# A fused attention and token-mixing kernel: first tiles loaded in halves, the ones of V written by GpSimd, longer planned transfers, another written order

## The chip, the cores and the metric

One Trainium2 chip, one core. The time is device microseconds of the whole program; the runs of a kernel agree within a fraction of a per cent. Shown times are medians of unprofiled runs. One further execution was recorded by the hardware profiler, and all rows below come from it. Engines: PE is TensorE's matmul stream and PEld its weight loads, DVE is VectorE, ACT is ScalarE, POOL is GpSimd, SP is SyncE, which only issues transfers here.

## What is computed

One sequence of 2048 tokens of width 512 in bf16. After a layer norm without weights, 32-head attention (16 values per head) and a token-mixing MLP (2048 tokens to 1376 and back) are computed side by side and added to the input:

```python
x = A_x
xn = _layernorm(x, axis=-1)
return x + _A_ref(xn, A_wqkv, A_wo) + _B_ref(xn, B_w1, B_b1, B_w2, B_b2)

# _A_ref, in short
q, k, v = heads of x @ wqkv            # 32 heads of 16
p = softmax(q @ k.T * 16 ** -0.5)      # over 2048 keys
return (p @ v) @ wo
# _B_ref, in short
h = _layernorm(x)
u = gelu(einsum("bsd,sf->bdf", h, w1) + b1)
return transpose(einsum("bdf,fs->bds", u, w2) + b2)
```

## The kernel before

**Blocks and groups.** Attention is cut into 32 blocks: 4 stretches of 512 queries by 8 sets of four heads. A block has 16 groups, one for each 128 keys; a group is four score matmuls (four heads, packed in the rows of the array, L557). There are 512 groups.

**Two ways for the exponential.** A group either goes to ScalarE, as two exponentials over 128x1024 (L565), or to VectorE, which builds the exponential out of the bits of a bf16 number: four instructions (one per head) write a first plane from the scores (`dve_first`, L612), and two more add a shift to the whole plane to give a second and a third plane (`add_plane`, L617). The planes together approximate the power of two. The product with V (L577) then takes four matmuls for a ScalarE group and three times four for a VectorE group, the third plane with weights scaled by 0.75 (V17b). V has a seventeenth column of ones beside each head's sixteen values, so that the same matmul sums the denominators; the ones are written once, at the start, by ScalarE (L407).

**A block's end.** When all products of a block stand in their PSUM bank, VectorE copies them (OT, L1093), so that the bank is free for the next block. A chain of small transfers on SP then takes the denominator rows to DRAM (`gather`), back in another layout (`gather2`), VectorE takes reciprocals (L1108), and they go out to DRAM and back, broadcast to four times 32 partitions (`bcast`). GpSimd multiplies the block by them (L1130). Blocks of odd number are joined into the same tile by four more transfers (`join`).

**The start.** Four x tiles of 128 tokens are loaded first, tile 0 and 2 by SP and tile 1 and 3 by ACT's queue (L401); then the first columns of the K and Q weights, then the rest. VectorE takes statistics of tile 0, 1 and 2 (L443, L445), GpSimd the power -1/2 (L453, L455), VectorE normalizes tile 0 (L463), takes tile 3's statistics and normalizes the others; TensorE transposes (L631), ScalarE or VectorE copies them out (L492, L494), TensorE projects K and Q for these tiles (L498), and the first scores and exponentials run while the other 12 tiles are prepared. Matmuls on zeros (L671, L1577) fill TensorE where the planner finds nothing else for it.

**A written order.** The program has no order of its own at run time: when it is built, a planner (class `Sched` and the dispatcher from L1696 on) walks a planned time, with an occupied time (`occ`) and a time to the result (`lat`) for each operation, and writes each engine's instructions in the order that comes out. Engines then run their lists in order and wait on semaphores. Which groups go to VectorE, and where each filler stands, falls out of this walk. `TOL` says by how much work put in between may make ScalarE's scores late; `JOIN` how long TensorE may wait for a VectorE bank, so that its scores go out together with ScalarE's; `KEEP0` how many matmul units TensorE is to have had in the last 3.4 us of planned time up to `T_KEEP0`, with zeros filled in otherwise. The planner also keeps GpSimd's long operations (`occ` above 1000, `wide`) and VectorE's plane steps and normalizations (`two`) apart: a GpSimd operation waits for the last such VectorE operation written before it, and VectorE's list places none inside a long GpSimd operation's planned time. Nothing makes VectorE wait for GpSimd at run time in this: if GpSimd starts later than planned, they run side by side.

**The tail.** After the last block VectorE transposes its sums, divides, and transposes back (L1734 to L1741), TensorE adds the output projection of the last pieces (L899, L907, L934), ScalarE and VectorE copy out four tiles, and SP stores them. Projection steps that don't need the last block are written into the list from the point at which the block before the last is planned to have been multiplied.

Of the kernel before, what the change touches and what calls it, by code (L numbers as in the profile page):

```python
# [8 lines left out]
ACTF = mybir.ActivationFunctionType  # L9
# [5 lines left out]
D = 512  # L15
H = 32
# [7 lines left out]
NKT = 16  # L24
# [233 lines left out]
def bass_parallel_sum__softmax_full_mha__mixer_token_mlp__prompt_kernel(  # L258
# [11 lines left out]
    x = A_x  # L270
    if len(x.shape) == 3:
        x2 = x.rearrange("b s d -> (b s) d")
        out2 = out.rearrange("b s d -> (b s) d")
    else:
        x2, out2 = x, out

    with ExitStack() as es:
# [8 lines left out]
        x_sb = x_flat[:, :].rearrange("p (t d) -> p t d", d=D)  # L286
# [10 lines left out]
        KT = sb("KT", [128, 4, S], BF16)  # L297
# [37 lines left out]
        PV_BANK = 6  # L335
# [21 lines left out]
        NPRE = 4  # L357
        TABLE = 1283.0


# [29 lines left out]
        def ld_x(a, b_, lat, q="sp"):  # L390
            dma(q, x_sb[:, a:b_, :],
                x2[128 * a:128 * b_, :].rearrange("(t p) d -> p t d", p=128),
                reads=[], writes=[("x", t) for t in range(a, b_)], name="ld_x", lat=lat)
# [7 lines left out]
        for t in range(NPRE):  # L401
            ld_x(t, t + 1, 2150 + 200 * (t // 2), "sp" if t % 2 == 0 else "act")
        ld_w(1, 0, 1, 3000, "sp")
        ld_w(0, 0, 1, 3100)
        sc.add("act", lambda e: e.activation(r2[:, 0:1], zw[:, 0:1], ACTF.Identity), reads=[("zw",)], writes=[("r2",)],
               occ=1500)
        sc.add("act", lambda e: e.activation(v17_views[0][1][:, :, 16], KT[:, 1, 0:NKT * H], ACTF.Identity, bias=1.0),  # L407
               reads=[("KTt", 1, t) for t in range(4)], writes=[("Vone",)], occ=490, lat=670)
        ld_x(4, 6, 4500)
# [32 lines left out]
        def ln_stats1(t):  # L442
            sc.add("dve", lambda e: e.bn_stats(stats[:, t, :], x_sb[:, t, :]),  # L443
                   reads=[("x", t)], writes=[("stats", t)], occ=650, lat=780)
            return sc.add("dve", lambda e: e.bn_aggr(mv[:, t, 0:2], stats[:, t, :]),  # L445
                          reads=[("stats", t)], writes=[("mv", t)], occ=105, lat=232)
# [242 lines left out]
        transpose_mm(2, 0, 0)  # L689
        ln_norm(3)  # L690
        xnT_evac(2, 1, 0, 0, "dve")
        qt0_mm(0, QB)
# [393 lines left out]
        def chain_epi(b):  # L1086
# [16 lines left out]
            def gather2():  # L1103
                return dma("sp", den_s[:, eb, :], den_dram[eb].rearrange("r (c e) -> (r c) e", e=16),
                           reads=[("dend", eb)], writes=[("den_s", eb)], name="den_i", noncontig=True, lat=3000)

# [8 lines left out]
            def bcast():  # L1115
                assert bc_done[0] == b
                bc_done[0] += 1
                for r in range(4):
                    op = dma("sp", denb[32 * r:32 * r + 32, :], rec_dram[eb][r:r + 1, :].broadcast_to([32, 512]),
                             reads=[("recd", eb)], writes=[("denb", r)], name="den_b", noncontig=True, lat=2500)  # L1120
                return op
# [288 lines left out]
        def pv_candidates(t):  # L1410
            b = pv_block[0]
            if b >= NBLK or not pv_open[0]:
                return []
            return [it for it in pv_items[b] if it[0] <= t and (
                b > 0 or (it[2] % NKT in (v0_done if it[1] == "A" else v0b_done) and v_ready(it) <= t))]
# [25 lines left out]

        TOL = 150.0
        JOIN = 45.0
        DEFER = 250.0
# [3 lines left out]
        def pe_fill(t, lim, same_cfg):  # L1448
            cands = []
            pvc = pv_candidates(t)  # L1450
            if pvc and sc.ready(writes=[("bank", PV_BANK)], eng="pe") <= t:
                it = min(pvc, key=lambda z: (z[1] == "D" and len(planes_avail()) > 1, z[0]))
                cands.append(("P", it))
# [137 lines left out]
        KEEP = 8.0  # L1591
        KEEP0, T_KEEP0 = 12.0, 25000.0
        n_zero = [0]
# [11 lines left out]

        D_HUNGRY = 0.0
        FAR = 1300.0
        n_act_ = [0]
# [233 lines left out]
```

## Time and profile before

| | us |
|---|---|
| median of three unprofiled runs | 698.42 |
| lowest and highest of them | 698.36, 699.23 |
| profiled execution | 701.9 |
| its span, first to last instruction | 700.1 |
| ScalarE busy | 683.0 |
| VectorE busy | 657.8 |
| TensorE busy (matmul stream) | 657.4 |
| GpSimd busy | 64.3 |

How to read the rows: a group of instructions stands as line, engine, operation, tile written, tile read, shapes and count, then busy time, the mean of one in ns, and the idle time of that engine just before these instructions, with what ended most of it. Instructions of one engine overlap at their ends, so the mean of one can be longer than its share of the busy time. A row of a timeline has the start, the length, the engine and line, how many instructions are merged, and in brackets the idle time before. The granted clock of TensorE is 1.00 at full speed and 0.50 when it is throttled.

### The profile page before, as it was taken

The page shows a single profiled execution, that of the slowest core. Times are in us where ns is not written, and L with a number is a line of the kernel's source. Part 1 is how long each engine was busy: PE and PEld are TensorE (multiplying, and loading weights), DVE is VectorE, ACT ScalarE, POOL GpSimd, SP SyncE. Part 2 cuts the span into 40 slices and gives each one's busy share as a digit, 9 for nine tenths or more (in the row PEclk, how much of TensorE's full clock was granted, in tenths as well). Part 3 has the DMA queues.
Part 4 walks back from the last instruction along what each step waited for, and adds up shares of the span by engine and source line. Part 5 has one row for each costly group of instructions (what it writes and reads, how often), then busy time and mean ns, then how long its engine had stood idle before and what let it go on. Part 6 is the DMA issues. An engine that isn't in the chain of part 4 may idle for free.

```text
span 700.1 us, 15532 instructions
## 1 busy us (share of the span) xinstructions
PE 657.4 (94%) x6195; PEld 198.4 (28%) x6277; DVE 657.8 (94%) x1139; ACT 683.0 (98%) x742; POOL 64.3 (9%) x93
## 2 busy tenths in 40 slices
PE   8999999999999999999999999989989999999987
PEld 4533333322222222222222222222222222222222
DVE  7888999999999999999999999998999999999997
ACT  7999999999999999999999999998999999999995
POOL 4510100000000000000000000000000000001000
PEclk9999999999999999999999999998999999999999
DMA  7024110022223221011222211111100122211001
GB/s 211 1 68 82 37 26 11 20 47 58 46 51 73 48 58 40 23 32 37 54 62 49 63 52 48 47 44 44 37 23 15 32 52 60 58 45 44 15 9 45
DMA packets 78367, 32.65 MB, mean 47 GB/s; under 512 B 63004, under 2 KB 74204, under 8 KB 78296
## 3 DMA queue, kind: packets, MB, share of 16 engines
q1 hardware_dynamic: 77480, 31.27, 18.4%
q8 instruction: 49, 0.80, 0.5%
q10 hardware_dynamic: 816, 0.39, 0.2%
q14 instruction: 22, 0.18, 0.1%
HBM read 26.08 MB, written 2.61 MB: 41 GB/s over the span
## 4 chain that ended last, share of the span: by engine, by line
ACT 84%; PE 9%; DVE 4%; issue 1%; POOL 0%; DMA 0%; DVEq 0%
ACT pT L565 83%; PE ps L557 3%; PE ps L577 3%; DVE x_sb L612 1%; PE ps L889 1%; ACT gT L880 1%; DVE plx L612 1%; PE ps L498 1%; DVE x_sb L617 1%; PE ps L899 1%; POOL r L480 0%; DMA x_sb<-in_A_x_dram 0%; DVE stats L443 0%; PE ps L631 0%; ACT QT L518 0%
## 5 line engine op out<-in xcount | busy, mean ns | idle before, releaser
L565 ACT ACTIVATE pT<-ps 128x1024 bf16<-128x1024 f32 x726 | 667.8, 1136 | 5.2 <-PE ps L557 4.9
L557 PE MATMUL ps<-QT,KT 32*128 32x512 bf16 x2048 | 291.0, 385 | 21.7 <-ACT pT L565 18.5
L612 DVE TENSOR_SCALAR x_sb<-ps 128x512 int16<-128x512 f32 x268 | 183.3, 686 | 12.0 <-PE ps L557 3.3
L612 DVE TENSOR_SCALAR plx<-ps 128x512 int16<-128x512 f32 x272 | 178.5, 682 | 3.6 <-PE ps L557 3.2
L557 PEld LDWEIGHTS ps<-QT,KT 32*128 32x128 bf16 x2048 | 73.9, 91 | 282.6 <-ACT pT L565 265.5
L577 PE MATMUL ps<-pT,V 128*32 128x512 bf16 x1452 | 143.6, 391 | 0.9 <-DVE OT L1093 0.6
L617 DVE TENSOR_SCALAR x_sb<-plx 128x2048 int16<-128x2048 int16 x90 | 61.3, 685 | 0.9 <-PE ps L577 0.6
L577 PEld LDWEIGHTS ps<-pT,V 128*32 128x32 bf16 x1452 | 36.5, 93 | 80.5 <-issue 74.3
L577 PE MATMUL ps<-plx,V 128*32 128x512 bf16 x556 | 54.0, 386 | 0.4
L577 PE MATMUL ps<-x_sb,V 128*32 128x512 bf16 x532 | 52.1, 388 | 1.7 <-DVE OT L1093 1.3
L889 PE MATMUL ps<-gT,w2blk 128*128 128x512 bf16 (+1 forms) x154 | 50.6, 385 | 3.1 <-issue 2.5
L858 PE MATMUL ps<-h_sb,w1blk 128*128 128x512 bf16 (+1 forms) x157 | 49.1, 385 | 2.7 <-issue 2.5
L1130 POOL TENSOR_TENSOR oT<-OT,denb 128x512 bf16<-128x512 f32 x16 | 20.3, 1271 | 337.0 <-DVE x_sb L617 173.6
L617 DVE TENSOR_SCALAR plx<-x_sb 128x2048 int16<-128x2048 int16 x71 | 48.7, 687 | 2.5 <-PE ps L577 2.2
L1130 POOL TENSOR_TENSOR otmp<-OT,denb 128x512 bf16<-128x512 f32 x15 | 19.1, 1271 | 263.3 <-DMA denb<-rec_scr 100.4
L498 PE MATMUL ps<-xnT,wqkv_sb 128*128 128x512 bf16 (+1 forms) x166 | 35.2, 305 | 3.6 <-issue 1.9
L577 PE MATMUL ps<-x_sb,V17b 128*32 128x512 bf16 x380 | 37.5, 385 | 0.5 <-issue 0.5
L617 DVE TENSOR_SCALAR x_sb<-x_sb 128x2048 int16<-128x2048 int16 x51 | 34.7, 686 | 1.4 <-PE ps L577 1.3
L612 DVE TENSOR_SCALAR xn_sb<-ps 128x512 int16<-128x512 f32 x48 | 32.9, 686 | 2.7 <-PE ps L557 0.8
L617 DVE TENSOR_SCALAR plx<-plx 128x2048 int16<-128x2048 int16 x32 | 21.9, 685 | 1.1 <-PE ps L577 0.8
L1093 DVE COPY OT<-ps 128x512 f32<-128x512 f32 x31 | 21.1, 680 | 0.1
L498 PE MATMUL ps<-wqkv_sb,xnT 128*128 128x128 bf16 x256 | 21.0, 220 | 0.2 <-issue 0.2
(103 smaller groups left out, 371.2 us busy)
## 6 DMA issues: line engine op xcount, KB each, us to landing
denb<-rec_scr SPq DMA_DIRECT2D x124, 64.0 KB, 2.1
w1blk<-in_B_w_dram SPq DMA_DIRECT2D x10, 512.0 KB, 4.1
w2blk<-in_B_w_dram SPq DMA_DIRECT2D x16, 320.0 KB, 3.4
xres<-in_A_x_dram SPq DMA_DIRECT2D x16, 128.0 KB, 2.4
QT<-qst SPq DMA_DIRECT2D x120, 16.0 KB, 1.8
out_dram<-osb SPq DMA_DIRECT2D x14, 128.0 KB, 1.7
wqkv_sb<-in_A_wqkv_dram SPq DMA_DIRECT2D x3, 384.0 KB, 7.6
x_sb<-in_A_x_dram SPq DMA_DIRECT2D x2, 512.0 KB, 6.9
```

Of the source, the lines that this page charges most:

```text
L498: return sc.add("pe", lambda e: e.matmul(dst, lhsT=lhsT, rhs=rhs, start=(ct == 0), stop=(ct == NCT - 1)), reads=reads, writes=[("bank", bk ...
L557: return sc.add("pe", lambda e: e.matmul(bank(bk), lhsT=KT[32 * r:32 * r + 32, T, 128 * kt:128 * (kt + 1)], rhs=QT[32 * r:32 * r + 32, slo ...
L565: return sc.add("act", lambda e: e.activation(pT[:, buf, :], ps[:, slot * 1024:(slot + 1) * 1024], ACTF.Exp, scale=EXP_SCALE), reads=[("ba ...
L577: return sc.add("pe", lambda e: e.matmul(bank(PV_BANK)[32 * r:32 * r + 32, :], lhsT=vt_[:, off:off + 32], rhs=rhs, start=start, stop=stop, ...
L612: return sc.add("dve", lambda e: e.tensor_scalar(plane_i[pb][:, 512 * r:512 * (r + 1)], bank(bk), BIAS, 0.0, ALU.add, ALU.max), reads=[("b ...
L617: return sc.add("dve", lambda e: e.tensor_scalar(plane_i[pb], plane_i[pb0], float(SHIFT[j]), BITS_MAX, ALU.add, ALU.min), reads=[("pl", pb ...
L858: op = sc.add("pe", lambda e: e.matmul(bank(xb)[0:m, :], lhsT=w1blk[:, slot, st, 0:m], rhs=h_sb[:, st, :], start=(st == 0), stop=(st == NT ...
L880: op = sc.add("act", lambda e, m=m, f0=f0, f1=f1: e.activation(gT[0:m, f0:f1, :], gT[0:m, f0:f1, :], ACTF.Gelu_apprx_tanh), reads=[("gT", ...
L889: op = sc.add("pe", lambda e: e.matmul(bank(xb), lhsT=w2blk[0:m, slot, ft, :], rhs=gT[0:m, ft, :], start=first, stop=last), reads=([("w2bl ...
L899: return sc.add("pe", lambda e: e.matmul(bank(bk), lhsT=oT[:, par, T, 128 * sti:128 * (sti + 1)], rhs=wo_c[:, T, :], start=first, stop=las ...
L1093: op = sc.add("dve", lambda e: e.tensor_copy(OT32[:, eb, :], bank(PV_BANK)), reads=[("bank", PV_BANK)], writes=[("OT32", eb)], **T_DVE(512))
L1130: op = sc.add("pool", lambda e: e.tensor_tensor(dst, OT32[:, eb, :], denb[:, :], ALU.mult), reads=[("OT32", eb)] + [("denb", r) for r in r ...
```

## The change

Each of the first four x tiles is loaded as two transfers of 64 partitions, the upper half by SP and the lower by ACT's queue, with a key of its own for the lower half, which the statistics now also wait for. ScalarE's activation that writes the ones of V is removed; a GpSimd memset of the same positions is written after the last of the first four normalizations. The planned landing of the denominators' second transfer goes from 3000 to 3500 ns and of the broadcast from 2500 to 3000 ns. `TOL` goes from 150 to 115, `JOIN` from 45 to 80, and `T_KEEP0` from 25000 to 70000 ns. Three more margins for the products with V (`PVM`, `PLM`, `PAM`) are added and set to zero. As the planner writes the order of all engines from these numbers, the whole order and the split of the groups can come out differently.

```diff
+        LAT_I, LAT_B = 3500.0, 3000.0
...
         for t in range(NPRE):
-            ld_x(t, t + 1, 2150 + 200 * (t // 2), "sp" if t % 2 == 0 else "act")
+            for i, q in enumerate(("sp", "act")):
+                dma(q, x_sb[64 * i:64 * i + 64, t, :], x2[128 * t + 64 * i:128 * t + 64 * i + 64, :], reads=[],
+                    writes=[("x", t)] if i == 0 else [("xh", t)], name="ld_x", lat=2150 + 150 * t)
...
-        sc.add("act", lambda e: e.activation(v17_views[0][1][:, :, 16], KT[:, 1, 0:NKT * H], ACTF.Identity, bias=1.0),
-               reads=[("KTt", 1, t) for t in range(4)], writes=[("Vone",)], occ=490, lat=670)
...
-                   reads=[("x", t)], writes=[("stats", t)], occ=650, lat=780)
+                   reads=[("x", t), ("xh", t)], writes=[("stats", t)], occ=650, lat=780)
...
         ln_norm(3)
+        sc.add("pool", lambda e: e.memset(v17_views[0][1][:, :, 16:17], 1.0), writes=[("Vone",)], occ=2300)
...
-                           reads=[("dend", eb)], writes=[("den_s", eb)], name="den_i", noncontig=True, lat=3000)
+                           reads=[("dend", eb)], writes=[("den_s", eb)], name="den_i", noncontig=True, lat=LAT_I)
...
-                             reads=[("recd", eb)], writes=[("denb", r)], name="den_b", noncontig=True, lat=2500)
+                             reads=[("recd", eb)], writes=[("denb", r)], name="den_b", noncontig=True, lat=LAT_B)
...
-            return [it for it in pv_items[b] if it[0] <= t and (
+            return [it for it in pv_items[b] if it[0] + (PLM if it[1] == "D" else PAM) <= t and (
...
-        TOL = 150.0
-        JOIN = 45.0
+        TOL = 115.0
+        JOIN = 80.0
...
-            if pvc and sc.ready(writes=[("bank", PV_BANK)], eng="pe") <= t:
+            if pvc and sc.ready(writes=[("bank", PV_BANK)], eng="pe") + PVM <= t:
...
-        KEEP0, T_KEEP0 = 12.0, 25000.0
+        KEEP0, T_KEEP0 = 12.0, 70000.0
...
+        PVM, PLM, PAM = 0.0, 0.0, 0.0
```

## The prediction

> **What bounds the kernel now.** I read the page's totals first, then the groups of ScalarE, then its instructions in order of time.
>
> ```profile
> span 700.1 us, 15532 instructions
> ...
> PE 657.4 (94%) x6195; PEld 198.4 (28%) x6277; DVE 657.8 (94%) x1139; ACT 683.0 (98%) x742; POOL 64.3 (9%) x93
> ...
> L565 ACT ACTIVATE pT<-ps 128x1024 bf16<-128x1024 f32 x726 | 667.8, 1136 | 5.2 <-PE ps L557 4.9
> ```
>
> The profiled execution took 701.9 us, 1.8 more than its span. ScalarE does 726 exponentials in 667.8 us, so 0.920 us each (the mean of 1.136 overlaps its neighbours), and has almost no idle time between them. A group of a block is two exponentials on ScalarE, or six instructions and no exponential on VectorE. The end is therefore the first exponential's start, plus 0.920 us for each, plus the gelu, plus the gaps, plus the tail. The gaps are few:
>
> ```profile
> 11.04 7.57 ACT L565 ACTIVATE pT<-ps 128x1024 bf16<-128x1024 f32 x8
> 19.00 9.27 ACT L565 ACTIVATE pT<-ps 128x1024 bf16<-128x1024 f32 x10 [0.39 <-PE ps L557]
> 29.02 280.13 ACT L565 ACTIVATE pT<-ps 128x1024 bf16<-128x1024 f32 x305 [0.75 <-PE ps L557]
> ...
> 471.59 1.02 ACT L565 ACTIVATE pT<-ps 128x1024 bf16<-128x1024 f32 x1 [1.45 <-PE ps L557]
> 473.10 1.02 ACT L565 ACTIVATE pT<-ps 128x1024 bf16<-128x1024 f32 x1 [0.49 <-PE ps L557]
> 474.61 1.02 ACT L565 ACTIVATE pT<-ps 128x1024 bf16<-128x1024 f32 x1 [0.49 <-PE ps L557]
> 476.55 215.09 ACT L565 ACTIVATE pT<-ps 128x1024 bf16<-128x1024 f32 x234 [0.92 <-PE ps L557]
> 695.76 1.09 ACT L492 ACTIVATE osb<-ps 128x512 bf16<-128x512 f32 x2 [4.12 <-PE ps L907]
> ```
>
> Four gaps between 470 and 477 us add up to 1.45 + 0.49 + 0.49 + 0.92 = 3.35 us; two near 19 and 29 us make 1.14. The last exponential ends at 691.64, 8.5 us before the span's end. What happened at 470 stands in the timeline around it and in the table by stretches:
>
> ```profile
> 466.17 1.27 POOL L1130 TENSOR_TENSOR otmp<-OT,denb 128x512 bf16<-128x512 f32 x1 [20.73 <-DMA denb<-rec_scr]
> 466.43 1.55 DVE L617 TENSOR_SCALAR xn_sb<-plx 128x2048 int16<-128x2048 int16 x1
> ...
> 470.39 0.11 PEld L577 LDWEIGHTS ps<-x_sb,V 128*32 128x32 bf16 x4 [1.33 <-DVE OT L1093]
> ```
>
> ```profile
> 75.00:469.00 394.00, 381.78 (x3553) 109.33 (x3596) 377.25 (x628) 393.51 (x426) 24.14 (x19) 1.00 0.19 45
> 469.00:477.00 8.00, 6.96 (x54) 1.30 (x53) 5.58 (x9) 4.66 (x6) 0.00 (x0) 0.57 0.04 9
> 477.00:690.00 213.00, 194.19 (x1883) 55.39 (x1903) 206.05 (x345) 212.90 (x233) 17.46 (x15) 1.00 0.15 37
> ```
>
> (Columns: length; busy time of PE, PEld, DVE, ACT, POOL; granted clock; DMA.) GpSimd's multiply waited for its denominators' transfer, started late, and ran beside a VectorE plane step, which took 1.55 us in place of 0.68. VectorE's copy of the finished block (L1093) came late, TensorE stood 1.33 us for it, its granted clock fell to a mean of 0.57, and ScalarE starved for 3.35 us.
>
> That is the key to the two times. 701.9 - 3.35 = 698.55 lies 0.13 from the median 698.42 of the unprofiled runs. So I take it that those runs mostly don't have this stall: it depends on when a transfer lands. The sum below is made on the profile without its stall, which agrees with the median, and a repaired stall gains nothing there.
>
> The Trainium skill's page "TensorE: Matmul & The Clock Gate" (Part 1: The HAM clock gate) lets the clock fall to half after an idle window of about 3.4 us. The trace differs: the pause was 1.33 us and the clock fell. By the page only the first wait of 1.45 would be lost, by the trace 3.35.
>
> **The start.** Now x tile 0 goes whole on SP and tile 1 whole on ACT's queue at the same moment.
>
> ```profile
> 0.74 0.90 ACTq L350 DMA_DIRECT2D x_sb<-in_A_x_dram  x2
> ...
> 3.61 0.69 DVE L443 BATCH_NORM_STATS2 stats<-x_sb 128x6 f32<-128x512 bf16 x1 [2.39 <-DMA x_sb<-in_A_x_dram]
> ...
> 4.44 0.66 DVE L443 BATCH_NORM_STATS2 stats<-x_sb 128x6 f32<-128x512 bf16 x1
> ```
>
> ```profile
> GB/s 0 0 0 0 0 0 0 0 0 0 0 0 0 0 0 0 0 0 0 0 0 0 0 27 55 68 150 164 164 259 287 314 314 246 300 273 287 232 232 219
> DMA packets 287, 0.27 MB, mean 90 GB/s; under 512 B 24, under 2 KB 287, under 8 KB 287
> ```
>
> (DMA view of the first 3 us; slices of 0.075 us.) By 3.0 us 0.27 MB have moved, about both tiles of 0.13 MB; half of it was there by the slice that ends at 2.48. With tile 0's halves ahead on both queues, tile 0 is complete some 0.5 us earlier, and VectorE's chain, which then runs without a DMA wait, with it: -0.5. Tile 1 is issued one slot of 0.45 us (0.90 for two) later and is wanted 0.83 us after tile 0 (3.61 to 4.44), so it isn't late. The first weights stand behind the same number of bytes on each queue as before.
>
> The Trainium skill's page "DMA: Bandwidth & Descriptors" (Rules for kernel authors) speaks against it: two transfers to disjoint halves of the partitions share the same engines and serialize, so one should not bother. By it this term is 0 and the sum 0.5 higher; it is a rival below.
>
> ScalarE issues five transfers in place of three, 0.9 us more before its table load. That would hurt if the activation that writes the ones stayed; it goes.
>
> ```profile
> 2.15 1.28 ACT L405 ACT_TABLE_LOAD   x1 [2.15 <-issue]
> 3.44 0.20 ACT L405 ACTIVATE r<-zw 128x1 f32<-128x1 bf16 x1
> 3.55 2.36 ACT L407 ACTIVATE V<-KT 128x512 bf16<-128x512 bf16 x1
> 6.90 0.60 ACT L492 ACTIVATE xnT<-ps 128x512 bf16<-128x512 bf16 x1 [0.98 <-PE ps L631]
> ```
>
> Without L407 ScalarE is free at 3.64 + 0.9 = 4.5, and is wanted at 6.90 - 0.5 = 6.4: the removal of 2.36 us is hidden by TensorE, worth 0 by itself. Had it stayed, ScalarE would be free at 6.8, 0.4 late.
>
> The ones now are a GpSimd memset, planned at 2300 ns, behind tile 3's statistics and the last of the first normalizations.
>
> ```profile
> 7.33 1.26 DVE L463 TENSOR_SCALAR xn_sb<-x_sb,mv 128x512 bf16<-128x512 bf16 x3
> ...
> 10.45 0.22 POOL L453 TENSOR_SCALAR mv<-mv 128x1 f32<-128x1 f32 x1 [2.31 <-DVE mv L445]
> ...
> L1193 POOL MEMSET QT<- 128x1024 bf16 x1 | 0.9, 946 | 0.0
> ```
>
> Its price is not in this trace. Lower bound: half of the dense 1024-element memset, 0.47 us; upper: the 2.36 us of ScalarE's same scattered 512 positions. It starts at 8.59 - 0.5 = 8.1 and ends at 8.6 to 10.5; GpSimd's next work, tile 4's statistics, is ready at 10.45 - 0.5 = 9.95. So tile 4 comes 0 to 0.5 us late, and behind it on GpSimd stand the statistics of all later tiles, which VectorE's normalizations and TensorE's transposes await. ScalarE already has its 0.39 gap at 18.6 for such keys, so nothing covers it. I take the scattered row as the nearer one, but VectorE can do other tiles' statistics meanwhile: +0.25.
>
> **Denominators.** Planned landings of two transfers grow by 0.5 us each; no instruction is added. GpSimd's multiply is planned 1 us later, and VectorE's plane steps are kept clear of the later place.
>
> ```profile
> POOL otmp L1130 <- DMA denb<-rec_scr: 100.4, 5, 26.3
> ...
> POOL oT L1130 <- DMA denb<-rec_scr: 59.9, 3, 21.8
> ```
>
> In 5 + 3 = 8 of 31 multiplies (one for each block but the last) the transfer still came last. One of these collided as above; the next worst plane step took 0.80 us, by the view of that line (least, median and longest ns):
>
> ```profile
> L617 DVE TENSOR_SCALAR plx<-x_sb x71: 631/684/798, 55.1 to 691.5; 128x2048 int16<-128x2048 int16 x71
> ...
> L617 DVE TENSOR_SCALAR xn_sb<-plx x12: 682/684/1555, 178.6 to 552.6; 128x2048 int16<-128x2048 int16 x12
> ```
>  The extra 1 us is hidden by GpSimd's own idle (20.73 us before the multiply quoted). At the end the cover is thin:
>
> ```profile
> 688.16 1.27 POOL L1130 TENSOR_TENSOR oT<-OT,denb 128x512 bf16<-128x512 f32 x1 [19.83 <-DVE x_sb L617]
> ...
> 694.37 0.71 DVE L1741 STREAM_TRANSPOSE otmp<-gT 128x512 bf16<-128x512 bf16 x1
> ...
> 694.91 0.38 PE L899 MATMUL ps<-wo_c,oT 128*128 128x512 bf16 x1
> 695.13 0.38 PE L907 MATMUL ps<-wo_pad,oT 128*128 128x512 bf16 x1
> ```
>
> VectorE's last transpose ends at 695.08, and TensorE's last output step that doesn't need it begins at 695.13: both arrive together. If one such step is planned behind the later multiply, the tail grows by one spacing of such steps, 694.91 to 695.13: +0.2, bounds 0 and +1.0 (the whole of the longer plan).
>
> **The order.** The tolerances (150 to 115, 45 to 80) change the whole written order and the split of groups. PVM, PLM, PAM are zero: nothing. The filler matmuls up to 70 us only take time that TensorE has free, and ScalarE has no gap from 29.02 on; cost 0, and 0.23 (two at half of one tolerance) if that cover fails, which changes no case.
>
> A group moved from ScalarE to VectorE saves 2 x 0.920 = 1.84 us. On VectorE it costs
>
> ```profile
> L612 DVE TENSOR_SCALAR x_sb<-ps 128x512 int16<-128x512 f32 x268 | 183.3, 686 | 12.0 <-PE ps L557 3.3
> L612 DVE TENSOR_SCALAR plx<-ps 128x512 int16<-128x512 f32 x272 | 178.5, 682 | 3.6 <-PE ps L557 3.2
> L617 DVE TENSOR_SCALAR x_sb<-plx 128x2048 int16<-128x2048 int16 x90 | 61.3, 685 | 0.9 <-PE ps L577 0.6
> ```
>
> 4 x 0.67 + 2 x 0.68 = 4.0 us. VectorE's idle time in the two undisturbed stretches is (394 - 377.25) + (213 - 206.05) = 23.7 us, room for five groups at most; 15.6 us of idle stand before the first-plane steps, which is what a wider joining of scores (80 ns) can fill. Against that, a tighter tolerance refuses TensorE fillers and pushes them together. Bounds: two groups more on VectorE (-3.7) to one fewer (+1.84). A quarter of the 15.6 us is one group, and I take that: -1.84.
>
> **Sum.** -0.5 + 0.25 + 0.2 - 1.84 = -1.9: 698.42 - 1.9 = 696.5 us. The profiled execution would go to 701.9 - 3.35 - 1.9 = 696.7.
>
> **The rivals.**
> The split stays. Then -0.05 is left: 698.4. For it: VectorE is 94% busy already; against: its idle before the first planes.
> The halves bring nothing because they share the transfer engines, and the split stays: 698.9. For it: the rate is 219 to 314 GB/s already in the later slices; against: today tile 0 shares them with tile 1.
> The timed runs do have the stall, and it goes, with the split unchanged: 698.42 - 0.05 - 3.35 = 695.0. Against: 698.55.
> Slower, by a collision of the new order: GpSimd's multiply starts beside a plane step that stands just ahead of a block's copy, in ordinary runs, and the clock falls: +3.35 - 0.05, so 701.7. It decides from the point where the copy makes TensorE stand about 1.3 us. For it: 8 of 31 transfers came last; against: only one of the eight did harm, and the plan now allows 1 us more.
> Slower, one group moves to ScalarE, because TensorE (94%) loses fillers to the tighter tolerance: 698.42 + 1.84 - 0.05 = 700.2.
>
> **How the numbers follow.** Forecast 0.40 (its own range 695.5 to 697.4); split stays 0.17; halves bring nothing 0.09; stall repaired 0.10; collision 0.15; a group more on ScalarE 0.09. A measurement of this kernel can tell about 0.2% (1.4 us) from no change. Faster: 0.40 + 0.10 = 0.50; within: 0.17 + 0.09 = 0.26; slower: 0.15 + 0.09 = 0.24. The range 694.2 to 700.6 holds all but the collision, with 0.8 below the stall case for a second group.
>
> **What would show it.** The start: first statistics at about 3.1, first exponential at 10.5. The ones: a GpSimd memset between 0.5 and 2.4 us, gap near 18 us no more than 0.7. The split: 724 exponentials. The plan: no plane step over 0.8 us, the clock at 1.00 through the whole middle. The tail: 8.5 to 8.9 us after the last exponential. I am wrong if the exponentials number 726 or more, or if ScalarE has a new gap over 1 us in the middle.

## The result, and the profile after

The changed kernel took 696.59 us (median of 8 runs, 696.16 to 697.93), the kernel before beside it 699.38 us (8 runs, 698.36 to 701.99): ratio 0.9958, 95% interval 0.9940 to 0.9976. It is faster by 2.8 us, 0.4%, which is clear of the noise; the forecast was 696.5. The three runs of before that the prediction started from were on the low side: in the 81 further runs of before in the experiments below (27 in each of three groups), the medians were 699.44, 698.94 and 699.29. The time outside the span is 1.8 us in nearly all executions (more in some of a2, d2, e1 and e3 below, up to 3.9), so spans are compared below where small things count.

The page of the profiled execution of after (697.93 us) has these totals and this group of exponentials. All line numbers are one to three higher than before.

```profile
span 696.1 us, 15540 instructions
...
PE 655.3 (94%) x6195; PEld 199.7 (29%) x6281; DVE 656.5 (94%) x1139; ACT 679.5 (98%) x741; POOL 66.3 (10%) x94
...
L566 ACT ACTIVATE pT<-ps 128x1024 bf16<-128x1024 f32 x726 | 666.6, 1146 | 1.3 <-PE ps L558 0.9
```

726 exponentials, as before: the split between ScalarE and VectorE did not move. The one ScalarE instruction fewer (741 for 742) is the removed L407. ScalarE in order of time:

```profile
3.91 1.28 ACT L408 ACT_TABLE_LOAD   x1 [3.91 <-issue]
...
7.22 0.60 ACT L493 ACTIVATE xnT<-ps 128x512 bf16<-128x512 bf16 x1 [1.82 <-PE ps L632]
...
12.28 7.44 ACT L566 ACTIVATE pT<-ps 128x1024 bf16<-128x1024 f32 x8
20.66 289.35 ACT L566 ACTIVATE pT<-ps 128x1024 bf16<-128x1024 f32 x315 [0.94 <-PE ps L558]
...
317.61 370.14 ACT L566 ACTIVATE pT<-ps 128x1024 bf16<-128x1024 f32 x403
691.81 1.08 ACT L493 ACTIVATE osb<-ps 128x512 bf16<-128x512 f32 x2 [4.06 <-PE ps L909]
```

The two spans differ by 700.1 - 696.1 = 4.0 us, and these rows say where. The first exponential is *later*: 12.28 for 11.04, +1.24. From there to the end of the last one (317.61 + 370.14 = 687.75) one gap is left, of 0.94. Before there were eight: the six that the prediction quoted, 4.49 us, and the two that stand here from ScalarE's timeline of before:

```profile
369.38 28.71 ACT L565 ACTIVATE pT<-ps 128x1024 bf16<-128x1024 f32 x31 [0.28 <-PE ps L557]
398.25 71.89 ACT L565 ACTIVATE pT<-ps 128x1024 bf16<-128x1024 f32 x78 [0.17 <-PE ps L557]
```

That makes 4.94 before and 0.94 after: -4.00, of which 3.35 is the stall near 470 and 0.65 the others. The exponentials and the gelu themselves took 1.13 us less. Of this 0.96 lies behind the gelu (370.14 us for 403 exponentials in place of 371.10), where the old order starts anew after six gaps: each new start loses the overlap with the instruction before (the three isolated exponentials at 471 to 476 us take 1.02 each, in a chain one costs 0.92). The tail from 687.75 to the end is 8.35 for 8.46: -0.11. Together 1.24 - 4.00 - 1.13 - 0.11 = -4.0.

The table by stretches (columns as in the prediction) has the clock at full where it had fallen to 0.57:

```profile
75.00:469.00 394.00, 380.37 (x3583) 109.58 (x3627) 379.38 (x636) 393.86 (x426) 24.93 (x20) 1.00 0.19 45
469.00:477.00 8.00, 7.36 (x77) 2.11 (x74) 7.79 (x14) 8.00 (x10) 0.00 (x0) 1.00 0.03 4
```

And no plane step is disturbed, in the view of that line (least, median, longest ns), while GpSimd's list of waits has half as many multiplies that wait for their denominators:

```profile
L618 DVE TENSOR_SCALAR plx<-x_sb x74: 625/682/789, 62.8 to 684.2; 128x2048 int16<-128x2048 int16 x74
```

```profile
POOL oT L1132 <- DMA denb<-rec_scr: 35.0, 2, 19.1
...
POOL otmp L1132 <- DMA denb<-rec_scr: 32.8, 2, 17.6
```

2 + 2 = 4 of 31 in place of 8, and 0.79 us is the longest step in place of 1.55. The start in the timeline:

```profile
0.74 2.50 ACTq L350 DMA_DIRECT2D x_sb<-in_A_x_dram  x4
...
1.26 4.02 PE L672 MATMUL ps<-KT,zw 128*128 128x512 bf16 x9 [1.26 <-DVE b1c_bf L421]
...
3.35 0.69 DVE L444 BATCH_NORM_STATS2 stats<-x_sb 128x6 f32<-128x512 bf16 x1 [2.12 <-DMA x_sb<-in_A_x_dram]
...
4.50 0.69 DVE L444 BATCH_NORM_STATS2 stats<-x_sb 128x6 f32<-128x512 bf16 x1 [0.24 <-DMA x_sb<-in_A_x_dram]
...
6.58 0.61 PE L632 MATMUL ps<-ident,xn_sb 128*128 128x128 bf16 x4 [1.29 <-DVE xn_sb L464]
...
8.76 2.28 POOL L692 MEMSET V<- 128x512 bf16 x1 [0.51 <-DVE xn_sb L464]
...
11.70 0.22 POOL L454 TENSOR_SCALAR mv<-mv 128x1 f32<-128x1 f32 x1 [0.66 <-DVE mv L446]
```

Tile 0's statistics start 0.26 us earlier than before (3.61), but tile 1 is now waited for (0.24), as the four half issues take 2.50 us on a queue, 0.62 each, where a whole tile took 0.45. Then the first transposes take 0.61 us for four, where the same four took 0.40 before: TensorE goes at half speed until about 10 us, and that puts the first exponential back. Five of the 8 runs have spans of 694.3 to 694.8, three, this profile among them, 695.9 to 696.1: two groups 1.3 us apart.

### The profile page after: what moved, and what is told of

The parts are those of the page before. It is cut to its first block, busy times and chain, and to the rows that moved or that the text cites. A ratio compares the mean times of both kernels' runs of the same rounds, so it can differ in the third digit from the quotient of the medians.

```text
span 696.1 us, 15540 instructions
## 1 busy us (share of the span) xinstructions
PE 655.3 (94%) x6195; PEld 199.7 (29%) x6281; DVE 656.5 (94%) x1139; ACT 679.5 (98%) x741; POOL 66.3 (10%) x94
## 4 chain that ended last, share of the span: by engine, by line
ACT 85%; PE 10%; DVE 4%; issue 1%; DMA 0%; DVEq 0%; SPq 0%
ACT pT L566 83%; PE ps L558 3%; PE ps L578 3%; PE ps L891 1%; PE ps L499 1%; DVE x_sb L613 1%; ACT gT L882 1%; DVE stats L444 1%; PE ps L901 1%; PE ps L632 0%; DMA x_sb<-in_A_x_dram 0%; DVE plx L613 0%; DVE xnT L495 0%; DVE xn_sb L464 0%; PE ps L909 0%
## 5 line engine op out<-in xcount | busy, mean ns | idle before, releaser
L613 DVE TENSOR_SCALAR x_sb<-ps 128x512 int16<-128x512 f32 x292 | 198.8, 683 | 14.2 <-PE ps L558 4.4
L613 DVE TENSOR_SCALAR plx<-ps 128x512 int16<-128x512 f32 x260 | 169.6, 679 | 1.3 <-PE ps L558 0.9
L618 DVE TENSOR_SCALAR x_sb<-plx 128x2048 int16<-128x2048 int16 x88 | 59.7, 682 | 1.4 <-PE ps L578 0.8
L578 PE MATMUL ps<-x_sb,V 128*32 128x512 bf16 x580 | 56.0, 382 | 0.8 <-issue 0.5
L618 DVE TENSOR_SCALAR plx<-x_sb 128x2048 int16<-128x2048 int16 x74 | 50.5, 685 | 2.7 <-PE ps L578 2.5
L891 PE MATMUL ps<-gT,w2blk 128*128 128x512 bf16 (+1 forms) x150 | 48.2, 384 | 3.3 <-issue 2.9
L618 DVE TENSOR_SCALAR x_sb<-x_sb 128x2048 int16<-128x2048 int16 x65 | 44.1, 681 | 0.2
L578 PE MATMUL ps<-x_sb,V17b 128*32 128x512 bf16 x368 | 36.0, 382 | 0.2 <-DVE x_sb L618 0.2
L613 DVE TENSOR_SCALAR xn_sb<-ps 128x512 int16<-128x512 f32 x44 | 30.1, 683 | 2.1 <-PE ps L558 0.7
```

Of the source, the lines that this page charges most:

```text
L578: return sc.add("pe", lambda e: e.matmul(bank(PV_BANK)[32 * r:32 * r + 32, :], lhsT=vt_[:, off:off + 32], rhs=rhs, start=start, stop=stop, ...
L613: return sc.add("dve", lambda e: e.tensor_scalar(plane_i[pb][:, 512 * r:512 * (r + 1)], bank(bk), BIAS, 0.0, ALU.add, ALU.max), reads=[("b ...
L618: return sc.add("dve", lambda e: e.tensor_scalar(plane_i[pb], plane_i[pb0], float(SHIFT[j]), BITS_MAX, ALU.add, ALU.min), reads=[("pl", pb ...
L891: op = sc.add("pe", lambda e: e.matmul(bank(xb), lhsT=w2blk[0:m, slot, ft, :], rhs=gT[0:m, ft, :], start=first, stop=last), reads=([("w2bl ...
```

## The experiments

The theory after the result: the gain comes from the collision of GpSimd's multiply with a plane step, which is in ordinary runs of before too, and from fewer other gaps; the start gives nothing. The rivals: the start gives it; the two landings by themselves do; or only this one written order does, which the numbers happened to draw. Each kernel was timed in five rounds beside the kernel before; kernels of one group of lines below ran on one chip and share the runs of before above them (6 runs of a2, b1 and e4, 10 or 12 of the others).

| kernel | median (lowest, highest) us | ratio to before [95%] | spans, median (lowest, highest) |
|---|---|---|---|
| before, 1st chip | 699.44 (697.91, 701.47) | | 697.6 (696.1, 699.6) |
| a1_start | 698.42 (698.04, 699.72) | 0.9990 [0.9981, 0.9999] | 696.6 (696.2, 697.9) |
| a2_order | 703.33 (701.94, 707.86) | 1.0063 [1.0039, 1.0087] | 700.95 (700.1, 705.8) |
| c1_short_before | 698.69 (696.84, 699.80) | 0.9984 [0.9972, 0.9995] | 696.9 (695.0, 698.0) |
| c2_short_after | 696.86 (696.14, 698.08) | 0.9967 [0.9954, 0.9980] | 695.0 (694.3, 696.2) |
| before, 2nd chip | 698.94 (697.70, 701.63) | | 697.1 (695.9, 699.8) |
| d1_whole | 696.37 (696.19, 696.57) | 0.9963 [0.9950, 0.9977] | 694.6 (694.4, 694.8) |
| d2_zeros | 696.54 (696.07, 697.69) | 0.9963 [0.9950, 0.9976] | 694.3 (694.2, 694.6) |
| b1_late_before | 707.92 (706.77, 711.29) | 1.0136 [1.0109, 1.0163] | 706.15 (705.0, 709.5) |
| b2_late_after | 699.58 (698.01, 701.25) | 1.0000 [0.9986, 1.0015] | 697.75 (696.2, 699.4) |
| before, 1st chip again | 699.29 (697.85, 701.68) | | 697.5 (696.0, 699.9) |
| e1_whole_zeros | 696.80 (696.38, 697.65) | 0.9962 [0.9947, 0.9977] | 694.6 (694.5, 694.8) |
| e2_old_landing | 700.48 (699.15, 701.29) | 1.0009 [0.9997, 1.0022] | 698.65 (697.3, 699.5) |
| e3_old_tol | 700.61 (699.68, 702.04) | 1.0015 [1.0003, 1.0027] | 698.5 (697.1, 700.2) |
| e4_late_old_landing | 708.59 (706.10, 710.15) | 1.0123 [1.0099, 1.0147] | 706.75 (704.3, 708.3) |

The after kernel's own spans were 694.7 (694.3, 696.1).

Each execution also left the mean of its granted clock. One stretch of 3.41 us at half speed, as in the trace of c1 below, gives 0.998; the profile of before, with 6.83 us, has 0.994. Of the 81 runs of before in the table, 33 have 0.997 or 0.998, with a median span of 698.1, and 48 have 0.999 or 1.0, with 696.6. All 12 spans of 699.0 or above are among the 33, and no run has 0.994. Of the 50 runs with after's order and no added transfer two have 0.998; that of c2's profile lies in the start, from 7.78 us. So falls of the clock are part of what the medians of before hold, but none as long as in the profile that the prediction read.

**The collision taken out of each order.** GpSimd's multiply works on 8 of the 512 columns, planned as long as before, so that the written order stays what it was; the rest of the product is left out.

```diff
-  e.tensor_tensor(dst, OT32[:, eb, :], denb[:, :], ALU.mult)
+  e.tensor_tensor(dst[:, 0:8], OT32[:, eb, 0:8], denb[:, 0:8], ALU.mult)
```

In the order of before:

> The kernel before in its own written order, with GpSimd's multiplies cut to 8 of 512 columns, so that most of the normalization is left out (the tiles are zeroed at the start instead). It takes the collision of GpSimd's multiply with VectorE's plane step away and nothing else. If the collision makes the stalls (theory A): median 696 to 698.4, spread under 1.5 us, no plane step over 0.85 us, no ScalarE gap over 1 us after 40 us. If the stalls have another cause (a late transfer or the clock by itself): median and spread as before, 699.4 and 3.6 us.

In the order of after:

> The changed kernel with the same cut (8 of 512 columns of each multiply). Theory A: no change against the changed kernel, 696 to 698, since nothing is left to collide. If collisions still cost there: over 0.5 us lower.

In the timeline of the first, around the place where before collided, the short multiply again starts just ahead of the plane step, and the step takes its usual time; ScalarE has no gap there:

```profile
466.45 0.20 POOL L1133 TENSOR_TENSOR otmp<-OT,denb 128x8 bf16<-128x8 f32 x1 [21.51 <-DMA denb<-rec_scr]
...
466.92 0.68 DVE L620 TENSOR_SCALAR xn_sb<-plx 128x2048 int16<-128x2048 int16 x1
...
671.75 0.55 PE L560 MATMUL ps<-QT,KT 32*128 32x512 bf16 x3 [0.49 <-ACT pT L568]
672.23 0.62 PE L580 MATMUL ps<-pT,V 128*32 128x512 bf16 x4
...
674.28 1.02 ACT L568 ACTIVATE pT<-ps 128x1024 bf16<-128x1024 f32 x1 [0.75 <-PE ps L560]
...
675.69 13.86 ACT L568 ACTIVATE pT<-ps 128x1024 bf16<-128x1024 f32 x15 [0.39 <-PE ps L560]
```

The order of before gains 0.7 us in the median span and 1.1 in the lowest one (696.1 to 695.0); the order of after gains nothing (lowest 694.3 in both). So the multiplies cost time beside VectorE in ordinary runs of before, and nothing of it is left in after; as all 31 multiplies are short here, this is the price of all of them, not of the place at 466 us alone. But it is under half of the 2.8: without it before is still 0.7 us behind in the lowest span (695.0 to 694.3). Some 0.5 of these 0.7 are gaps: c1's profile still has those of 0.39, 0.75 and 0.28 us where after has the one of 0.94. The rest isn't assigned.

Theory A is borne out only in part. It expected a median of at most 698.4 and a spread under 1.5 us, and these are 698.69 and 2.96. The clock falls in this order without a collision: 5 of the 12 runs still have 0.998, and the rows at 672 us show one such fall with no multiply near. In the table by stretches of c1 and then of before, over just the time at half speed:

```profile
671.85:675.26 3.41, 3.41 (x24) 0.62 (x22) 2.83 (x5) 2.66 (x3) 0.00 (x0) 0.50 0.03 5
```

```profile
470.17:477.00 6.83, 6.61 (x52) 1.25 (x52) 4.45 (x8) 3.52 (x4) 0.00 (x0) 0.50 0.03 5
```

**The start alone, in the order of before.** The halves, the added key and the memset in the kernel before (in the traces its order is that of before from 53 us on; ahead of that 13 of VectorE's instructions and some groups of TensorE's stand elsewhere):

```diff
-            ld_x(t, t + 1, 2150 + 200 * (t // 2), "sp" if t % 2 == 0 else "act")
+            for i, q in enumerate(("sp", "act")):
+                dma(q, x_sb[64 * i:64 * i + 64, t, :], ...
-        sc.add("act", lambda e: e.activation(v17_views[0][1][:, :, 16], ...
+        sc.add("pool", lambda e: e.memset(v17_views[0][1][:, :, 16:17], 1.0), writes=[("Vone",)], occ=2300)
```

> The kernel before with the start alone changed (halves on two queues, ones by GpSimd); its written order is that of before but for some 40 of 1900 rows on TensorE. Theory A (the gain is the stall in the middle, which the new order avoids): the median stays within 1 us of before's 699.4, some executions over 700.5 as before, and the profile, if it falls on such a one, has a plane step over 1.2 us and ScalarE gaps of 2 us or more near 470 us; the first exponential at 11 to 12.3 us. Theory B (the start is worth 0.5 us or more): 0.5 to 1 us below before in the same rounds, first exponential at 10.5 to 10.8.

The lowest span gains nothing (696.2 for 696.1). The median is 1.0 lower, with an interval that reaches to 0.9999. Neither theory fits as a whole: the first exponential, at 12.06, is theory A's, but no run lies above 700.5, where theory A expected some. What is missing is the long executions. None of the 12 has a granted clock under 0.999, while 11 of the 27 of before beside them have; these 11 have a median span of 698.0 and the other 16 one of 696.8, near the 696.6 of a1. So the new start, or the steps that it moves ahead of 53 us, takes these falls of the clock away; by what isn't shown. The timeline shows the collision still there, in its milder form:

```profile
467.08 1.27 POOL L1131 TENSOR_TENSOR otmp<-OT,denb 128x512 bf16<-128x512 f32 x1 [20.65 <-DMA denb<-rec_scr]
...
467.40 1.49 DVE L617 TENSOR_SCALAR xn_sb<-plx 128x2048 int16<-128x2048 int16 x1
...
470.94 0.40 PE L577 MATMUL ps<-x_sb,V 128*32 128x512 bf16 x4 [0.69 <-DVE OT L1094]
...
471.71 1.02 ACT L565 ACTIVATE pT<-ps 128x1024 bf16<-128x1024 f32 x1 [0.59 <-PE ps L557]
```

The plane step takes 1.49 us, the block's copy is late, TensorE stands 0.69 us, but its four matmuls then take 0.40: the clock held, and ScalarE lost 0.59 where the profile of before lost 3.35. There, in the timeline of before, the same four took 0.62:

```profile
470.39 0.62 PE L577 MATMUL ps<-x_sb,V 128*32 128x512 bf16 x4 [1.03 <-DVE OT L1093]
```

**The start undone in the order of after.** First the whole tiles back, with all else, the order too, as in after:

```diff
-            for i, q in enumerate(("sp", "act")):
-                dma(q, x_sb[64 * i:64 * i + 64, t, :], ...
+            ld_x(t, t + 1, 2150 + 200 * (t // 2), "sp" if t % 2 == 0 else "act")
-                   reads=[("x", t), ("xh", t)], writes=[("stats", t)], occ=650, lat=780)
+                   reads=[("x", t)], writes=[("stats", t)], occ=650, lat=780)
```

> The changed kernel, every engine's written order the same, but the first four x tiles loaded whole again (two on each queue). If the halves are worth the 0.3 us by which the first statistics began earlier in the changed kernel's profile: 0.2 to 0.5 slower than the changed kernel's 696.6. If their doubled number of issues costs more (ScalarE's table load at 3.91 in place of 2.15 us, the first weights issued at 3.3 to 3.6 in place of 1.7): 0.3 to 0.8 faster, first exponential up to 1 us earlier at the same clock. By the rule that halves share the engines: no difference within 0.2.

Then the halves kept, and 12 filler matmuls ahead of the first transposes in place of 9, so that TensorE has hardly a pause there:

```diff
-        zeros(9, 430)
+        zeros(12, 430)
```

> The changed kernel in its order with three more filler matmuls at the start (12 in place of 9), so that TensorE works from 1.3 to 6.5 us without the pause from 5.3 to 6.6. If the two groups of times (696.2 to 696.6 and 697.5 to 698.1) come from the clock that TensorE has between 6.6 and 10 us: nearly all executions in the lower group, median 696.2 to 696.5, the transposes and projections there at 0.22 us for four in place of 0.43. If they come from the transfers at the start: both groups stay.

Then both, the fillers planned at 322.5 ns each:

> The changed kernel in its written order with whole tiles and three more filler matmuls at the start. If both earlier runs add up as spans: all executions within 0.4 us of each other, span 694.2 to 694.6, so 696.0 to 696.4 if the 1.8 us around the span stay. If the fillers are what brings more time around the span (1.8 to 3.3 us in the run with 12 fillers): 696.1 to 697.7 again.

TensorE's and ScalarE's timelines at the start, first with whole tiles, then with 12 fillers:

```profile
1.26 3.56 PE L670 MATMUL ps<-KT,zw 128*128 128x512 bf16 x9 [1.26 <-DVE b1c_bf L419]
...
6.25 0.40 PE L630 MATMUL ps<-ident,xn_sb 128*128 128x128 bf16 x4 [1.43 <-DVE xn_sb L462]
...
10.82 7.44 ACT L564 ACTIVATE pT<-ps 128x1024 bf16<-128x1024 f32 x8
```

```profile
1.26 4.68 PE L672 MATMUL ps<-KT,zw 128*128 128x512 bf16 x12 [1.26 <-DVE b1c_bf L421]
...
6.15 0.40 PE L632 MATMUL ps<-ident,xn_sb 128*128 128x128 bf16 x4 [0.21 <-DVE xn_sb L464]
...
10.72 7.44 ACT L566 ACTIVATE pT<-ps 128x1024 bf16<-128x1024 f32 x8
```

For comparison c1, whose tiles are whole, in the timeline of TensorE:

```profile
6.29 0.61 PE L634 MATMUL ps<-ident,xn_sb 128*128 128x128 bf16 x4 [1.01 <-DVE xn_sb L466]
```

Whole tiles are as fast as halves: median span 694.6 for 694.7, and all of after's gain stays (0.9963). With 12 fillers, halves or whole, the group of spans near 696 is gone: all 22 executions end at 694.2 to 694.8. So the two groups of after come from TensorE's clock in its first 10 us, and a pause of 0.21 in place of 1.29 us ahead of the transposes avoids the later one. In the whole times the fillers bring nothing (696.54 and 696.80), as the time outside the span rose to 1.8 to 3.3 us in these two kernels; why wasn't found. d1 shows 10 such spans with the long pause left, 1.43 us; c1, with whole tiles too and 1.01, was at half speed. In after's order with 9 fillers, 8 of 18 executions with halves lie in the later group (3 of after, 5 of c2) and none of d1's 10 with whole tiles. So halves may make the start at half speed more likely; no run separates this from chance and from c2's added work at the start.

**The order numbers without the new start.** `TOL`, `JOIN`, `T_KEEP0` and the landings of after in the kernel before:

```diff
-        TOL = 150.0
-        JOIN = 45.0
+        TOL = 115.0
+        JOIN = 80.0
```

> The kernel before with the planner's numbers alone changed (both tolerances, filler limit, planned landings), start as before. Theory A: 696 to 697, spread under 2 us, 726 exponentials or very near, gaps of ScalarE after the first exponential under 2 us in sum. Theory B: within 1 us of before. A third way (the order gains by its split and not by the stall): fewer than 726 exponentials, 1.84 us for each two.

The same numbers draw another order from the old start, and it is 4 us slower than before, which none of the three ways expected. ScalarE has 2.83 us of wait at one place and again 726 exponentials:

```profile
36.49 276.13 ACT L565 ACTIVATE pT<-ps 128x1024 bf16<-128x1024 f32 x301 [0.94 <-PE ps L557]
...
373.58 317.32 ACT L565 ACTIVATE pT<-ps 128x1024 bf16<-128x1024 f32 x346 [2.83 <-PE ps L557]
```

There VectorE adds a tile of another stage (L978, from 371.48) ahead of the block's copy (L1093, from 372.08), and TensorE stands 1.12 us for the copy. The longest plane step is 0.97 us: this is no collision.

**One half of the order numbers undone in after.** The old landings, order drawn anew:

```diff
-        LAT_I, LAT_B = 3500.0, 3000.0
+        LAT_I, LAT_B = 3000.0, 2500.0
```

> The changed kernel with the old planned landings of the denominators' transfers (3000 and 2500 ns), all else as changed; the planner writes another order. If the longer landings make the gain: 1 to 3 us slower than the changed kernel, with a plane step over 1.1 us and several multiplies more that start by their transfer. If any redrawn order can be as good: within 0.5 us of it. If the changed order is a chosen one among unequal ones: slower for gaps that have nothing to do with a collision.

And the old `TOL`, `JOIN` and `T_KEEP0`, with the landings of after:

> The changed kernel with the old tolerances and the old filler limit, the new start and the longer landings. If the landings make the gain: 696.5 to 697.5, no plane step over 0.9 us. If the tolerances matter by themselves: slower than that, with ScalarE gaps of more than 2 us in sum where no multiply is near.

Each alone loses the whole gain (spans 698.65 and 698.5, for 697.5 of before), but by different ways. The profile of the first is one of its shorter executions, 697.4. Its longest plane step takes 1.21 us, so a collision is back, but ScalarE has no gap there. ScalarE ends its exponentials at 693.02 - 6.47 = 686.55 and waits 6.47 us in the tail, because plane steps and their matmuls of the last block run on until 690.3:

```profile
688.76 0.69 DVE L618 TENSOR_SCALAR x_sb<-plx 128x2048 int16<-128x2048 int16 x1
...
689.87 0.40 PE L578 MATMUL ps<-x_sb,V17b 128*32 128x512 bf16 x4
...
693.02 1.09 ACT L493 ACTIVATE osb<-ps 128x512 bf16<-128x512 f32 x2 [6.47 <-PE ps L909]
```

The second has no plane step over 0.79 us, and one gap of 2.40, at the same place as a2. There too VectorE has an addition of another stage queued ahead of the block's copy, and TensorE stands for the copy:

```profile
371.11 0.69 DVE L980 TENSOR_TENSOR osb<-ps,xres 128x512 bf16<-128x512 f32 x1
371.71 0.68 DVE L1095 COPY OT<-ps 128x512 f32<-128x512 f32 x1
...
372.45 0.10 PEld L578 LDWEIGHTS ps<-pT,V 128*32 128x32 bf16 x4 [1.60 <-DVE OT L1095]
372.45 0.40 PE L578 MATMUL ps<-pT,V 128*32 128x512 bf16 x4 [1.30 <-DVE OT L1095]
...
373.21 3.77 ACT L566 ACTIVATE pT<-ps 128x1024 bf16<-128x1024 f32 x4 [2.40 <-PE ps L558]
```

**Transfers made late.** One more real transfer between DRAM buffers in each block's chain of denominators, 1.9 us from issue to landing, which the planner takes as nothing, so that each order stays:

```diff
+                sc.add("sp", hop, reads=[("recd", eb)], writes=[("recd2", eb)], name="den_h", dma=True, occ=0.0, lat=0.0)
                 for r in range(4):
-                    op = dma("sp", denb[32 * r:32 * r + 32, :], rec_dram[eb][r:r + 1, :].broadcast_to([32, 512]),
+                    op = dma("sp", denb[32 * r:32 * r + 32, :], rec2_dram[eb][r:r + 1, :].broadcast_to([32, 512]),
```

In the order of before:

> The kernel before in its written order with one more real hop through DRAM in each denominators' chain, some 2 us, that the planner gives no time. Theory A: most of the 31 multiplies now start by their transfer, several run beside plane steps, and at places that stand ahead of a block's copy this costs 0.6 to 4 us each: 2 to 10 us slower than before. If late multiplies are harmless as a rule: within 1 us of before.

In the order of after:

> The same hop in the changed kernel. If its longer planned landings make it robust: half of the loss of the kernel before or less. If the order only happened to avoid a collision at the landings of today: as great a loss as before's, 2 to 10 us.

In the order of e2, which has after's tolerances and the old landings:

> The order of the changed kernel with old landings, with the extra hop of some 2 us in each denominators' chain. If the longer planned landings make an order robust: it loses about as much to the hop as the kernel before (8 to 10 us against the same kernel without it), against 3 for the changed kernel. If the loss hangs on the single order: anything from 1 to 10.

The added transfer in the list of DMA issues of b2 (queue, count, KB, median us to landing), and GpSimd's waits for denominators, in before's order and then in after's:

```profile
rec_scr<-rec_scr SPq DMA_DIRECT2D x31, 8.0 KB, 1.9
```

```profile
POOL oT L1136 <- DMA denb<-rec_scr: 296.1, 14, 31.2
POOL otmp L1136 <- DMA denb<-rec_scr: 218.4, 12, 25.3
```

```profile
POOL otmp L1138 <- DMA denb<-rec_scr: 212.5, 12, 24.3
POOL oT L1138 <- DMA denb<-rec_scr: 193.2, 9, 32.9
```

The price in the median span is 706.15 - 697.1 = 9.0 us for the order of before (its own spans on that chip), 706.75 - 698.65 = 8.1 for e2's and 697.75 - 694.7 = 3.0 for after's. The two orders with the old landings pay alike, the one with the longer landings a third. So after's tolerances alone don't make an order hold with late transfers, and the 1 us in the plan is what is left; but only one order with the longer landings was tried, and the hop was not put into e3's. After's order is not immune: 21 of 31 multiplies wait for the transfer, and the longest plane step takes 1.60 us:

```profile
L619 DVE TENSOR_SCALAR x_sb<-xn_sb x11: 674/682/1601, 151.3 to 603.6; 128x2048 int16<-128x2048 int16 x11
```

## Why the prediction was right, and where it was wrong

The side was right, and the number, 696.5 for 696.59, was right by luck: the base of the sum was 1.0 too low (698.42 for 699.38) and the gain 0.9 too small (1.9 for 2.8), and the two cancel. The gain came mostly from what the prediction had put at nothing. It had itself named its test, wrong if the exponentials number 726 or more. They number 726.

- **"A repaired stall gains nothing there"** failed, and with it the base of the sum. 701.9 - 3.35 = 698.55 fitted the median of three runs by chance; larger samples have 698.9 to 699.4. In its long form the stall is indeed not in those runs: none of 81 has the profile's clock of 0.994. But a milder one is. ScalarE loses 0.59 us where the clock holds (a1), and with the multiplies short the lowest span is 1.1 lower, the median 0.7 (c1). The step that failed is reading a subtraction that agrees with a median as proof that an event is absent, as if the stall were either there whole or not at all.
- **The halves, -0.5:** mis-sized. The first statistics came at 3.35, not 3.1, and whole tiles in the same order had them at 3.40 (d1). No time is gained: d1 and after are equal, and a1 has the lowest span of before. The rule of the Trainium skill's page "DMA: Bandwidth & Descriptors" (Rules for kernel authors), by which halves of the partitions gain nothing, gave the right term, and the runs agree. The prediction overlooked that a half takes longer to issue than a whole tile, 0.62 us for 0.45, with twice as many on each queue: tile 1 is late by 0.24, and ScalarE's table load starts at 3.91, 1.8 later and not 0.9.
- **First exponential at 10.5:** 12.28 in the profile, 10.72 to 10.82 where TensorE was at full speed (d2, d1). The prediction had no term for the clock at the start.
- **L407 removed, 0:** right. ScalarE waits 1.82 us for TensorE before its first evacuation.
- **GpSimd's memset, 0.47 to 2.36, +0.25:** the duration, 2.28, lies near the upper bound, as argued. The gap near 18 us was 0.94, not under the 0.7 that was named. In a1, in the order of before, it is 0.94 too, where c1 with the old start has 0.39 from as late a first exponential; so the new start lengthens it by 0.55, twice the term; in after it stands in place of two gaps that made 1.14. Whether the memset does this isn't shown: tile 4's statistics have 0.66 us of idle GpSimd time ahead of them in after's profile, and none in d1's, where TensorE started at full speed.
- **Longer landings, hidden, tail +0.2:** hidden, right; no plane step over 0.8 and the clock at 1.00 throughout, right. The tail is 8.35 for 8.46, below the 8.5 to 8.9 that was named: the 0.2 isn't seen.
- **One group more on VectorE, -1.84:** wrong, the split stayed. In its place stand the multiplies beside VectorE (1.1 in the lowest span), the other gaps (some 0.5 to 0.7) and fewer falls of the clock. The nearest to the mechanism was the rival "the timed runs do have the stall, and it goes", with the split unchanged; its price of 3.35 in the median was too high.
- **The collision of a new order** did not come in after. Its deciding point, TensorE standing about 1.3 us, doesn't hold: in e3 it stood 1.60 before the weight load and the clock stayed at full speed. And a2, e2 and e3 show orders from nearly the same numbers that lose 3.8 to 6.3 us against after (median spans), in a2 and e3 by a copy that makes TensorE stand 1.12 and 1.30 us without any collision.
- **Two readings that change no case:** ScalarE had two more gaps in the profile of before, 0.28 and 0.17, and 0.23 for the fillers is two whole tolerances of 0.115, not two halves.

What stays open: the last 1 us of the 2.8 in the medians is a matter of how often the longer executions occur (12 of 81 spans of before lie at 699.0 or above, none of 50 in the kernels with after's order and no added transfer lies above 696.2). The granted clocks put it down to falls of the clock, in 33 of the 81 and 2 of the 50. Why they occur in the order of before, and why the new start alone ended them in a1, isn't shown; that the start gives nothing holds for the lowest spans only. How many executions start with TensorE at half speed can't be read from this figure: after's profile, at half speed for its first 10 us, has 1.00. No run clearly beats after: d1 and d2 are equal to it within their intervals.

## What to carry to other kernels

A subtraction that lands on a median doesn't show that an event is missing from ordinary runs: look at the spread of more runs, or take the event out and measure. In a kernel with a written order, any planner number redraws the whole, and the gain belongs to the order drawn, not to the number; test a part by keeping the order fixed and changing only what happens on the chip. Margins for late transfers show their worth only when transfers are made late: 3.0 us lost in place of 9.0 here.

## What the runs showed of the hardware

- The length of TensorE's pause alone does not decide whether its clock falls. It fell in a pause of 1.03 us without a matmul (1.33 before the weight load) in the profile of before, at 470.17 us and so before the pause ended, and near 672 us in c1 after pauses of at most half a microsecond; it held after 0.69 in a1, after 1.12 in a2 and after 1.30 (1.60 before the weight load) in e3. The page "TensorE: Matmul & The Clock Gate" of the Trainium skill (Part 1: The HAM clock gate) asks for an idle window of about 3.4 us, which none of these pauses has.
- The time at half speed came in equal pieces: 3.41 us in c1, in b2 (from 591.41), in e4 (from 648.50) and in c2 (from 7.78), 6.83 in the profile of before. If the clock is set in steps of this length, it matters where in a step a pause lies; no run tests this.
- The table's granted clock is 1.00 in after's first 10 us too, where the transposes show half speed: 0.61 us for four in place of 0.40. There the time of equal groups of matmuls is the better witness.
- A half tile takes longer to issue than a whole one, 0.62 us for 0.45. GpSimd's memset of 512 scattered elements for each partition took 2.28 us, its dense one of 1024 elements 0.95.
